# Conditional weight fetches of a mixture-of-experts stage: the next expert is asked for when the current one starts

## The chip, the cores and the metric

The kernel runs on one core of a Trainium2 chip. A time is the device time of one execution in microseconds (us). Before the change three runs gave 460.19, 461.05 and 462.98 us; the median is 461.05.

## The reference, cut to what matters

Three layers follow one another, all in f32: a chunked attention (2 batches, 8 heads, 768 positions, 8 memory keys), a channel mix with three weight matrices, and a mixture of experts whose routing is sticky. The last one is where the change lies:

```python
for b in range(B):
    prev_e = -1
    for s in range(S):
        fresh_e = int(np.argmax(logits[b, s]))
        e = fresh_e if s == 0 or local_gate[b, s] < 0.5 else (prev_e if prev_e >= 0 else fresh_e)
        prev_e = e
        h = np.maximum(x[b, s] @ w1[e], 0.0)          # 512 x 1024
        out[b, s] = softmax(logits[b, s])[e] * (h @ w2[e])   # 1024 x 512
```

So each of 1536 rows passes one of 8 experts, and which one is known only when all logits are there. An expert's two matrices are 2 MB each.

## The kernel before

**Layers.** Attention and channel mix run in four units of 384 rows, on an order that a planner of the program lays out. Each finished row of the channel mix and its expert probability is written to `ys` in DRAM. The expert stage starts while the last unit is routed, at about 255 us.

**Slots.** The rows of an expert are packed into full slots of 128 rows and, for a remainder of at most 64, half slots. `tab_a`, `tab_e`, `tab_b` and `tab_c` (small operations on VectorE and a few on TensorE) work out tables: `ei[0, s]` is the expert of slot `s` (25 entries: 17 full, 8 half), `ei[1, s]` a flag that is 1 where a slot's expert differs from the slot before, `gix` the rows to gather and `six` the rows to store to. With these inputs there are 11 full slots (0 to 10) and 5 half slots. Experts change at slots 4, 8 and 9. Half slots 0 to 4 are taken behind slots 3, 5, 7, 8 and 9 (`HALF_AT`).

**A full slot** (`slot_body`, L1135): the rows come by an indirect DMA of GpSimd's queue into one of three buffers `yg` (`gather`, L855), are transposed on TensorE (`tx`, L866, L871), and go through two matrix products, each as three passes of high and low parts (`s1`, L876; `s2`, L896), with a transpose between (`th`, L889, L893). ScalarE and VectorE split every transposed tile into high and low (`split4`, L862: L863 and L864). `put` (L906) scales the result into `ot[0]`, and `store` (L910) scatters it from GpSimd's queue in the middle of the next slot.

**A half slot** (`half_body`, L1161) does the same for 64 rows without the split, straight from raw weights; all of it, its store, gather and weight fetch included, stands under `tc.If(nh > ...)` (L1183).

**Weights.** Three pairs of raw buffers exist. `raw[0]` holds what the next full slot's expert brings; `raw[1]` and `raw[2]` serve the half slots in turn. `w_fetch(s, k)` (L846) issues matrix `k` of slot `s` from SP's queue with `cond=fv`, the slot's flag: with a flag of 0 the instruction is issued and moves nothing. `w_part(s, part)` (L835) stands under a condition on the same flag; its four `w_piece` calls split a quarter of the raw weights into high (ScalarE, L828) and low (VectorE, L831). In `slot_body(s)` the next slot's first matrix is split between `s2`'s parts (`w_part(s + 1, 0)` and `w_part(s + 1, 1)`), its second in `slot_body(s + 1)` (parts 2 and 3). `h_fetch(h)` (L1067) loads the pair of half slot `h`.

**Order.** From L1051 on the order of each engine's instructions is the program's own (`manual_schedule`). Each queue runs in order: an instruction that waits holds back all behind it. The program's framework places the waits by reads and writes of buffers; a fetch under a condition counts as a write of its buffer. Ahead of the slots SP issues `w_fetch(2, 0)`, `h_fetch(0)` and `h_fetch(1)` (L1130, L1199, L1200). In the slots, SP's order is

```python
w_fetch(s + 1, 1)      # in slot_body(s), behind w_part(s, 3)
w_fetch(s + 2, 0)      # behind w_part(s + 1, 1)
h_fetch(h + 2)         # at the end of half_body(h)
```

Of the kernel before, what the change touches and what calls it, by code (L numbers as in the profile page):

```python
# [9 lines left out]
F32 = mybir.dt.float32  # L10
F32R = mybir.dt.float32r
BF16 = mybir.dt.bfloat16
I32 = mybir.dt.int32
U32 = mybir.dt.uint32
U64 = mybir.dt.uint64
ACTF = mybir.ActivationFunctionType
ALU = mybir.AluOpType
AX = mybir.AxisListType.X
ET = mybir.EngineType

B, H, S, D = 2, 8, 768, 64
CHUNK, LCTX, RCTX, NMEM = 32, 16, 8, 8
DM, DF, NE = 512, 1024, 8
P = 128
# [12 lines left out]
NFULL = 17  # L37
# [3 lines left out]
HALF_AT = (3, 5, 7, 8, 9, 11, 13, 15)  # L41
# [102 lines left out]
def kernel(  # L144
# [15 lines left out]
    nc = tc.nc  # L160
    SCALE = 1.0 / float(D) ** 0.5

    dram = ctx.enter_context(tc.tile_pool(name="dram", bufs=1, space=bass.MemoryType.DRAM))
    cp = ctx.enter_context(tc.tile_pool(name="cp", bufs=1))
    psum = ctx.enter_context(tc.tile_pool(name="psum", bufs=1, space=bass.MemoryType.PSUM))
    ys = dram.tile([B * S + 1, YW], F32, name="ys")


    banks = []
# [50 lines left out]
    stock = {}  # L220
# [21 lines left out]
    ones8 = c_sb[0:NE, 208:336]  # L242
# [444 lines left out]
    for u in range(NU):  # L687
# [4 lines left out]
        if u > 1:  # L692
            for i in range(H // 2):
                att_pair(u * H // 2 + i, T - 19 + 4.0 * i)
            for c in range(NC):
                ev = T - 20 + 2 * (2 * c + 1) + 4.15
# [26 lines left out]

    w1_s, w2_s = wk_s, wv_s
    hbuf, xbuf = wr_s[0:2], wr_s[2:4]
    raw, yg, hv, ot = {}, {}, {}, {}
    tri2 = cp.tile([NE, 16], F32, name="tri2")
    two1 = cp.tile([NE, 1], F32, name="two1")
    gix = cp.tile([P, NSLOT], I32, name="gix")
# [1 line left out]
    sixl = cp.tile([P, 1], I32, name="sixl")  # L731
    ei = cp.tile([1, 2, NSLOT + 3], I32, name="ei")
    fsel = cp.tile([1, 1], I32, name="fsel")

    def open_right():
        att_ctx.close()
        rw = ctx.enter_context(tc.tile_pool(name="rw", bufs=1, side="right"))
        raw[0] = (rw.tile([P, NC, DF], F32, name="raw1_0"), rw.tile([P, NF, DM], F32, name="raw2_0"))
        for k in range(3):
            yg[k] = rw.tile([P, YW], F32, name=f"yg{k}")  # L740
        for k in range(2):
            hv[k] = rw.tile([P, DM], F32, name=f"hv{k}")
# [92 lines left out]
    def w_part(s, part):  # L835
        if s < 2 or s >= NFULL:
            return
        k = (s, body[0] if s > NMIN and body[0] >= NMIN else 0)
        if k not in flag:
            flag[k] = nc.values_load(ei[0:1, 1, s:s + 1], engines=(ET.DVE, ET.Activation),  # L840
                                     min_val=0, max_val=1)
        with tc.If(flag[k]):  # L842
            for c in range(4):
                w_piece(s, part, c, nc.vector)

    def w_fetch(s, k):  # L846

        if s >= NFULL:
            return
        ev = nc.values_load(ei[0:1, 0, s:s + 1], engines=(ET.SP,), min_val=0, max_val=NE - 1)  # L850
        fv = nc.values_load(ei[0:1, 1, s:s + 1], engines=(ET.SP,), min_val=0, max_val=1)
        nc.sync.dma_start(out=raw[0][k], in_=(w1, w2)[k][bass.ds(ev, 1)].rearrange("o (c p) f -> p (o c) f", p=P),
                          cond=fv)

# [19 lines left out]
    def s1(s, g, cs):  # L874
        xh, xl = xbuf[s % 2]
        pb = banks[g]  # L876
        for c in cs:
            wh, wl = w1_s[c][g]
            sl = slice(c * P, (c + 1) * P)
            nc.tensor.matmul(pb, lhsT=xh[:, sl], rhs=wh, start=(c == 0), stop=False)  # L880
            nc.tensor.matmul(pb, lhsT=xh[:, sl], rhs=wl, start=False, stop=False)  # L881
            nc.tensor.matmul(pb, lhsT=xl[:, sl], rhs=wh, start=False, stop=(c == NC - 1))  # L882

    def relu(s, g, on_act):
        if on_act:
            nc.scalar.activation(out=hv[g], in_=banks[g], func=ACTF.Relu)
        else:
            nc.vector.tensor_scalar(out=hv[g], in0=banks[g], scalar1=0.0, scalar2=None, op0=ALU.max)
# [17 lines left out]
    def put(s):  # L906
        nc.scalar.activation(out=ot[0], in_=banks[2 + s % 2], func=ACTF.Copy, scale=yg[s % 3][:, DM:DM + 1])
        nc.vector.tensor_copy(sixl, six[:, s:s + 1])

    def store():  # L910

        nc.gpsimd.indirect_dma_start(out=out, out_offset=bass.IndirectOffsetOnAxis(ap=sixl, axis=0),  # L912
                                     in_=ot[0], in_offset=None, bounds_check=B * S - 1, oob_is_err=False)
# [17 lines left out]
    ef = cp.tile([1, NSLOT + 3], F32, name="ef")  # L931
# [91 lines left out]
    def tab_r():  # L1023
# [4 lines left out]
        nc.vector.tensor_reduce(out=hl[:, NE:], in_=hl[:, 0:NE], op=ALU.max, axis=AX)  # L1028
        nc.vector.tensor_tensor(out=ei[:, 0, NSLOT + 2:], in0=hl[:, NE:], in1=nfull, op=ALU.is_ge)


    u = NU - 1
    T = 20.0 * NU + 0.1
# [8 lines left out]
        (9.0, w_piece, 0, 3, 1, nc.gpsimd), (9.1, w_piece, 0, 3, 2, nc.gpsimd), (9.2, w_piece, 0, 3, 3, nc.gpsimd),  # L1042
        (9.5, tab_a), (10.0, route_c, u), (10.8, th, 0, 1), (11.2, s2, 0, range(0, 4)), (11.3, tab_e), (11.5, tab_b),
        (14.5, s2, 0, range(4, 8)), (15.0, s1, 1, 0, range(0, 4)), (15.1, relu, 1, 0, True), (15.2, tab_c),
        (15.3, gather, 2), (15.4, tab_r),
    ]
    for it in order:
        at(T + it[0], *it[1:])
# [5 lines left out]
    ep = ctx.enter_context(tc.tile_pool(name="ep", bufs=1))  # L1054
    raw[1] = (ep.tile([P, NC, DF], F32, name="raw1_1"), ep.tile([P, NF, DM], F32, name="raw2_1"))
    raw[2] = (ep.tile([P, NC, DF], F32, name="raw1_2"), ep.tile([P, NF, DM], F32, name="raw2_2"))
    for k in range(2):
        ot[k] = ep.tile([P, DM], F32, name=f"ot{k}")
    yh = [ep.tile([P, YW], F32, name=f"yh{k}") for k in range(2)]
    xh4 = [ep.tile([P, 4 * 64], F32, name=f"xh{k}") for k in range(2)]  # L1060
    hh4 = [ep.tile([P, 2 * P], F32, name=f"hh{k}") for k in range(2)]
# [5 lines left out]
    def h_fetch(h):  # L1067
        if h >= NE:
            return
        s = NFULL + h  # L1070
        ev = nc.values_load(ei[0:1, 0, s:s + 1], engines=(ET.SP,), min_val=0, max_val=NE - 1)
        fv = nc.values_load(ei[0:1, 1, s:s + 1], engines=(ET.SP,), min_val=0, max_val=1)
        r1, r2 = raw[1 + h % 2]
        nc.sync.dma_start(out=r1, in_=w1[bass.ds(ev, 1)].rearrange("o (c p) f -> p (o c) f", p=P), cond=fv)
        nc.sync.dma_start(out=r2, in_=w2[bass.ds(ev, 1)].rearrange("o (c p) f -> p (o c) f", p=P), cond=fv)

    def h_gather(h):
        if h < NE:
            nc.gpsimd.indirect_dma_start(out=yh[h % 2], out_offset=None, in_=ys[0:1 + B * S, :],
                                         in_offset=bass.IndirectOffsetOnAxis(ap=gix[:, NFULL + h:NFULL + h + 1], axis=0))  # L1080
# [32 lines left out]
    def h_s2(h, q, ks):  # L1113
        r2 = raw[1 + h % 2][1]
        for k in ks:
            for t in range(2):
                f = 4 * t + 2 * q + k
                for d in range(2):
                    nc.tensor.matmul(banks[2 + h % 2][d * 64:(d + 1) * 64, 0:256],
                                     lhsT=hh4[q][:, k * P + t * 64:k * P + (t + 1) * 64],  # L1120
                                     rhs=r2[:, f, d * 256:(d + 1) * 256], start=(q + k + t == 0), stop=(q + k + t == 3))

    def h_store(h):
        o = ot[1][:, h % 2 * 256:(h % 2 + 1) * 256]
        nc.scalar.activation(out=o, in_=banks[2 + h % 2][:, 0:256], func=ACTF.Copy, scale=yh[h % 2][:, DM:DM + 1])
        s = NFULL + h
        nc.gpsimd.indirect_dma_start(out=outh, out_offset=bass.IndirectOffsetOnAxis(ap=six[:, s:s + 1], axis=0),
                                     in_=o, in_offset=None, bounds_check=2 * B * S - 1, oob_is_err=False)

    w_fetch(2, 0)  # L1130
    put(0)
    nv = nc.values_load(ei[0:1, 0, NSLOT:NSLOT + 1], min_val=0, max_val=NFULL)
    nh = nc.values_load(ei[0:1, 0, NSLOT + 1:NSLOT + 2], min_val=0, max_val=NE)
# [1 line left out]
    def slot_body(s):  # L1135
        body[0] = s
        if s > 1:
            s1(s, 0, range(4))
            w_part(s, 2)
            relu(s, 0, True)  # L1140
        s1(s, 1, range(0, 2))
        th(s, 0)
        s1(s, 1, range(2, 4))
        relu(s, 1, False)
        w_part(s, 3)
        w_fetch(s + 1, 1)
        store()
        gather(s + 2)
        s2(s, range(0, 2))
        if s in HALF_AT:  # L1150
            h_tx(HALF_AT.index(s))
        th(s, 1)
        s2(s, range(2, 4))
        w_part(s + 1, 0)
        tx(s + 1)
        w_part(s + 1, 1)
        w_fetch(s + 2, 0)
        s2(s, range(4, 8))
        put(s)

    def half_body(h):  # L1161
        h_s1(h, 0, range(NC))
        h_relu(0)
        h_s1(h, 1, range(0, 2))
        h_th(h, 0)
        h_s1(h, 1, range(2, NC))
        h_relu(1)
        h_s2(h, 0, range(0, 1))
        h_th(h, 1)
        h_s2(h, 0, range(1, 2))  # L1170
        h_s2(h, 1, range(0, 2))
        h_store(h)
        h_gather(h + 2)
        h_fetch(h + 2)


    def slots(s):
        slot_body(s)
        if s == 1:
            h_gather(0)  # L1180
            h_gather(1)
        if s in HALF_AT:
            with tc.If(nh > HALF_AT.index(s)):  # L1183
                half_body(HALF_AT.index(s))
        if s < NMIN - 1:
            slots(s + 1)
        elif s < NFULL - 1:
            with tc.If(nv > s + 1):
                slots(s + 1)

    def half_rest(h):
        if h < NE:
            with tc.If(nh > h):
                with tc.If(nv < HALF_AT[h] + 1):
                    h_tx(h)
                    half_body(h)
                half_rest(h + 1)

    h_fetch(0)  # L1199
    h_fetch(1)  # L1200
    slots(1)
    nr = nc.values_load(ei[0:1, 0, NSLOT + 2:NSLOT + 3], min_val=0, max_val=1)
# [84 lines left out]
```

## Time and profile before

| What | Value |
|---|---|
| runs | 460.19, 461.05, 462.98 us |
| the profiled execution: own time, span | 459.79 us, 458.0 us |
| TensorE (PE) busy | 414.9 us of the span, 91% |
| VectorE (DVE), ScalarE (ACT), GpSimd (POOL) busy | 251.0, 187.3, 94.2 us |
| mean granted TensorE clock | 0.994 |
| SP's weight loads in the expert stage (`raw`) | 2048 KB each |
| HBM read | 109.40 MB |

The profiled execution's span runs from the first instruction to the last; its own time is 1.8 us longer. A busy PE says that matmuls were in its pipeline, not that it ran at its peak, so what it waited for is read from the lists of waits and from the timeline. SP has no busy time in the table; its instructions are DMA issues, register loads and waits.

### The profile page before, as it was taken

To read this page: it belongs to the slowest core of one execution; us is meant where nothing else is said; L and a number is where in the kernel's file an instruction comes from. 1 tells how busy PE (TensorE), PEld (TensorE's weight loads), DVE (VectorE), ACT (ScalarE), POOL (GpSimd) and SP (SyncE) were. 2 spreads that over 40 slices of the span, in tenths; PEclk is the share of its full clock that TensorE was granted. 3 is DMA by queue.
4 is the path that set the end of the run, shared out by engine and by line. 5 is a ranking of instruction groups with operands and counts; after the bars stand their busy time and mean duration, and the time that the engine had idled before them with its cause. 6 is when DMAs were issued, how large, how long until landed. Compare 5 with 4: busy or idle time off the path is not lost. (4 is left out here: it accounts for less than half of the span.)

```text
span 458.0 us, 10040 instructions
## 1 busy us (share of the span) xinstructions
PE 414.9 (91%) x3827; PEld 351.1 (77%) x3827; DVE 251.0 (55%) x628; ACT 187.3 (41%) x425; POOL 94.2 (21%) x96
## 2 busy tenths in 40 slices
PE   0557999999999999999999899997999999999992
PEld 0436899988999989997999777875786786767672
DVE  4999999835665466646642485225332116474310
ACT  3664995345420553204442231225432126465211
POOL 2312110412300221002320704110130130123030
PEclk9999999999999999999999999999999999999997
DMA  8989860224221020000561026997760897993020
GB/s 277 409 307 333 348 206 1 72 76 134 89 89 36 30 77 2 1 1 24 201 223 37 1 69 216 396 399 299 257 219 10 289 316 253 370 393 124 9 78 24
DMA packets 28096, 76.67 MB, mean 167 GB/s; under 512 B 3819, under 2 KB 3951, under 8 KB 28032
## 3 DMA queue, kind: packets, MB, share of 16 engines
q1 hardware_dynamic: 25216, 67.39, 40.6%
q0 software_dynamic: 2816, 8.47, 5.5%
q8 instruction: 34, 0.56, 0.5%
q14 instruction: 30, 0.25, 0.2%
HBM read 109.40 MB, written 6.69 MB: 254 GB/s over the span
## 5 line engine op out<-in xcount | busy, mean ns | idle before, releaser
L864 DVE TENSOR_TENSOR w<-bank,w 128x512 fp32r<-128x512 f32 x34 | 23.5, 690 | 73.3 <-ACTq L842 57.0
L479 PE MATMUL bank<-xkh,w 128*128 128x384 f32 x128 | 46.9, 366 | 1.2 <-ACT tmp L499 0.9
L211 POOL TENSOR_TENSOR k2l<-tmp,k2h 128x384 fp32r<-128x384 f32 x25 | 27.1, 1085 | 101.0 <-DVE k2h L208 63.8
L480 PE MATMUL bank<-xkl,w 128*128 128x384 f32 x128 | 44.1, 344 | 1.0 <-DVE xkl L211 1.0
L479 PE MATMUL bank<-k2h,w 128*128 128x384 f32 x128 | 44.6, 349 | 0.0
L831 DVE TENSOR_TENSOR w<-raw,w 128x512 fp32r<-128x512 f32 x56 | 35.7, 696 | 15.5 <-ACT w L828 15.2
L481 PE MATMUL bank<-xkh,w 128*128 128x384 f32 x128 | 43.9, 343 | 0.0
L481 PE MATMUL bank<-k2h,w 128*128 128x384 f32 x128 | 43.0, 336 | 0.0
L480 PE MATMUL bank<-k2l,w 128*128 128x384 f32 x128 | 42.9, 335 | 0.0
L863 ACT ACTIVATE w<-bank 128x512 fp32r<-128x512 f32 x34 | 20.3, 597 | 54.3 <-PE bank L893 32.7
L828 ACT ACTIVATE w<-raw 128x512 fp32r<-128x512 f32 x64 | 35.2, 621 | 4.6 <-DMA raw<-in_w_dram 4.3
L880 PE MATMUL bank<-w,w 128*128 128x512 f32 x88 | 36.3, 412 | 0.5 <-issue 0.5
L902 PE MATMUL bank<-w,w 128*128 128x512 f32 x88 | 36.4, 414 | 0.0
L882 PE MATMUL bank<-w,w 128*128 128x512 f32 x88 | 34.6, 394 | 0.0
L881 PE MATMUL bank<-w,w 128*128 128x512 f32 x88 | 34.6, 393 | 0.0
L904 PE MATMUL bank<-w,w 128*128 128x512 f32 x88 | 34.6, 393 | 0.0
L903 PE MATMUL bank<-w,w 128*128 128x512 f32 x88 | 34.4, 390 | 0.0
L381 ACT ACTIVATE Pm<-bank,mx 128x64 f32<-128x64 f32 x96 | 21.3, 322 | 21.8 <-DVE mx L372 21.3
L505 ACT ACTIVATE tmp<-bank 128x384 f32<-128x384 f32 x24 | 11.9, 494 | 41.5 <-PE bank L481 38.8
L479 PEld LDWEIGHTS bank<-xkh,w 128*128 128x128 f32 x128 | 24.8, 194 | 4.4 <-issue 1.9
L480 PEld LDWEIGHTS bank<-xkl,w 128*128 128x128 f32 x128 | 24.8, 194 | 1.4 <-DVE xkl L211 1.4
L481 PEld LDWEIGHTS bank<-xkh,w 128*128 128x128 f32 x128 | 24.7, 193 | 0.0
(214 smaller groups left out, 898.0 us busy)
## 6 DMA issues: line engine op xcount, KB each, us to landing
raw<-in_w_dram SPq DMA_DIRECT2D x36, 2048.0 KB
qk<-in_qkx_dram SPq DMA_DIRECT2D x16, 576.0 KB
vt<-in_vx_dram SPq DMA_DIRECT2D x16, 390.0 KB
w<-in_wk_dram SPq DMA_DIRECT2D x8, 512.0 KB
w<-in_wv_dram SPq DMA_DIRECT2D x8, 512.0 KB
ys<-yr SPq DMA_DIRECT2D x12, 256.0 KB
w<-in_wr_dram SPq DMA_DIRECT2D x4, 512.0 KB
raw<-in_w_dram SPq DMA_DIRECT2D x2, 1024.0 KB
```

The source lines that it names most:

```text
L211: (nc.vector if e == "d" else nc.gpsimd).tensor_tensor(out=o, in0=a, in1=b, op=op)
L479: nc.tensor.matmul(o[:, :UT], lhsT=wh, rhs=xh, start=first, stop=False)
L480: nc.tensor.matmul(o[:, :UT], lhsT=wh, rhs=xl, start=False, stop=False)
L481: nc.tensor.matmul(o[:, :UT], lhsT=wl, rhs=xh, start=False, stop=last)
L828: nc.scalar.activation(out=hi, in_=src, func=ACTF.Copy)
L831: lo_on.tensor_tensor(out=lo, in0=src, in1=hi.bitcast(F32), op=ALU.subtract)
L880: nc.tensor.matmul(pb, lhsT=xh[:, sl], rhs=wh, start=(c == 0), stop=False)
L881: nc.tensor.matmul(pb, lhsT=xh[:, sl], rhs=wl, start=False, stop=False)
L882: nc.tensor.matmul(pb, lhsT=xl[:, sl], rhs=wh, start=False, stop=(c == NC - 1))
L902: nc.tensor.matmul(pb, lhsT=hh[:, sl], rhs=wh, start=(c == 0), stop=False)
L903: nc.tensor.matmul(pb, lhsT=hh[:, sl], rhs=wl, start=False, stop=False)
L904: nc.tensor.matmul(pb, lhsT=hl[:, sl], rhs=wh, start=False, stop=(c == NF - 1))
```

## The change

Five things change.

1. `tab_n`, nine small VectorE operations planned between `gather(2)` and `tab_r`, makes a table `nx`: for a slot whose expert is new, `nx[0, s]` is the next new expert behind it and `nx[1, s]` is 1 if there is one; elsewhere `nx[1, s]` is 0.
2. `w_fetch(s, k)` reads `nx` instead of `ei`, so a fetch "of slot s" loads the expert that follows slot `s`'s, as soon as slot `s`'s own raw weights are split. In `slot_body(s)` the calls are `w_fetch(s, 1)` for `s > 1` and `w_fetch(s + 1, 0)` for `s > 0`.
3. Ahead of the slots SP issues a four-byte DMA from `yg[2]` to a DRAM tile `mark`, which waits for `gather(2)` to land; then `h_fetch(0)`, `w_fetch(0, 0)`, `w_fetch(0, 1)`, `h_fetch(1)`. The early `w_fetch(2, 0)` goes.
4. The half slot's store, gather and fetch leave the condition (`half_end`); its scaling stays in it (`h_put`) and writes one of two tiles `oh`, cleared once by GpSimd.
5. Where a half slot follows a full slot, the full slot's `store()` is issued between the half's arithmetic and `half_end`, and no longer in the next slot.

```diff
     def w_fetch(s, k):
         if s >= NFULL:
             return
-        ev = nc.values_load(ei[0:1, 0, s:s + 1], engines=(ET.SP,), min_val=0, max_val=NE - 1)
-        fv = nc.values_load(ei[0:1, 1, s:s + 1], engines=(ET.SP,), min_val=0, max_val=1)
+        ev = nc.values_load(nx[0:1, 0, s:s + 1], engines=(ET.SP,), min_val=0, max_val=NE - 1)
+        fv = nc.values_load(nx[0:1, 1, s:s + 1], engines=(ET.SP,), min_val=0, max_val=1)
...
+    def tab_n():
+        nm = stock["tmp"][0][0:1, 0:NFULL * NFULL].rearrange("p (a b) -> p a b", b=NFULL)
+        v = stock["tmp"][1][0:1, 0:5 * NFULL].rearrange("p (a b) -> p a b", b=NFULL)
+        rk, fe, fl = v[:, 0:2], v[:, 2:4], v[:, 4]
+        s2d = [1, NFULL, NFULL]
+        nc.vector.tensor_copy(fl, ei[:, 1, 0:NFULL])
+        nc.vector.tensor_tensor_scan(out=rk[:, 0], data0=ones8[0:1, 0:NFULL], data1=fl, initial=0.0, op0=ALU.mult, op1=ALU.add)
+        nc.vector.tensor_scalar(out=rk[:, 1], in0=rk[:, 0], scalar1=1.0, scalar2=None, op0=ALU.add)
+        nc.vector.tensor_tensor(out=fe[:, 0], in0=ef[:, 1:NFULL + 1], in1=fl, op=ALU.mult)
+        nc.vector.tensor_tensor(out=nm, in0=rk[:, 1].unsqueeze(2).to_broadcast(s2d), in1=rk[:, 0].unsqueeze(1).to_broadcast(s2d),
+                                op=ALU.is_equal)
+        nc.vector.tensor_tensor(out=nm, in0=nm, in1=fe[:, 0].unsqueeze(1).to_broadcast(s2d), op=ALU.mult)
+        nc.vector.tensor_reduce(out=fe[:, 1], in_=nm, op=ALU.add, axis=AX)
+        nc.vector.tensor_copy(nx[:, 0], fe[:, 1])
+        nc.vector.scalar_tensor_tensor(out=nx[:, 1], in0=rk[:, 0], scalar=rk[:, 0, NFULL - 1:], in1=fl, op0=ALU.is_lt,
+                                       op1=ALU.mult)
...
-        (15.3, gather, 2), (15.4, tab_r),
+        (15.3, gather, 2), (15.35, tab_n), (15.4, tab_r),
...
+    def h_put(h):
+        nc.scalar.activation(out=oh[h % 2], in_=banks[2 + h % 2][:, 0:256], func=ACTF.Copy,
+                             scale=yh[h % 2][:, DM:DM + 1])
...
-    w_fetch(2, 0)
     put(0)
...
         w_part(s, 3)
-        w_fetch(s + 1, 1)
-        store()
+        if s > 1:
+            w_fetch(s, 1)
+        if s - 1 not in HALF_AT:
+            store()
         gather(s + 2)
...
         w_part(s + 1, 1)
-        w_fetch(s + 2, 0)
+        if s > 0:
+            w_fetch(s + 1, 0)
         s2(s, range(4, 8))
         put(s)
...
         h_s2(h, 1, range(0, 2))
+        h_put(h)
+
+    def half_end(h):
         h_store(h)
         h_gather(h + 2)
         h_fetch(h + 2)
...
             h_gather(1)
+            for k in range(2):
+                nc.gpsimd.memset(oh[k], 0.0)
         if s in HALF_AT:
             with tc.If(nh > HALF_AT.index(s)):
                 half_body(HALF_AT.index(s))
+            store()
+            half_end(HALF_AT.index(s))
...
+    nc.sync.dma_start(out=mark, in_=yg[2][0:1, 0:1])
     h_fetch(0)
+    w_fetch(0, 0)
+    w_fetch(0, 1)
     h_fetch(1)
     slots(1)
```

## Rows read from the trace of the kernel before

**Rows 1.** The page, part 1 and part 2: busy time of PE; DMA share in 40 slices.
```profile
PE 414.9 (91%) x3827; PEld 351.1 (77%) x3827; DVE 251.0 (55%) x628; ACT 187.3 (41%) x425; POOL 94.2 (21%) x96
DMA  8989860224221020000561026997760897993020
```

**Rows 2.** Waits of PE, 215 to 458 us: us in total, times, longest us.
```profile
PE bank L1107 <- ACT hv L1100: 2.8, 1, 2.8
PE bank L893 <- ACT xh L1088: 2.4, 5, 0.5
PE bank L871 <- DMA yg<-ys,gix: 0.5, 1, 0.5
```

**Rows 3.** Timeline of PE, half slot 0: start, us, what, count, idle before and its releaser.
```profile
314.56 2.81 PE L1094 MATMUL bank<-raw,xh 128*64 128x256 f32 x24
320.17 0.44 PE L1107 MATMUL bank<-ident,hv 128*128 128x128 f32 x2 [2.80 <-ACT hv L1100]
```

**Rows 4.** Timeline of PE, half slot 2.
```profile
385.59 2.81 PE L1094 MATMUL bank<-raw,xh 128*64 128x256 f32 x24
388.33 0.44 PE L1107 MATMUL bank<-ident,hv 128*128 128x128 f32 x2
```

**Rows 5.** Timeline of ACT, slots 3, 7 and 9: splits of new weights, and half slot 0.
```profile
310.14 0.60 ACT L863 ACTIVATE w<-bank 128x512 fp32r<-128x512 f32 x1 [0.81 <-PE bank L893]
314.52 2.19 ACT L828 ACTIVATE w<-raw 128x512 fp32r<-128x512 f32 x4 [3.78 <-DMA raw<-in_w_dram]
319.74 0.37 ACT L1100 ACTIVATE hv<-bank 128x256 f32<-128x256 f32 x1
...
381.67 2.20 ACT L828 ACTIVATE w<-raw 128x512 fp32r<-128x512 f32 x4
...
416.26 2.19 ACT L828 ACTIVATE w<-raw 128x512 fp32r<-128x512 f32 x4 [0.25 <-ACT ot L1125]
```

**Rows 6.** Waits of SP's queue, 309 to 316 us.
```profile
SPq L852 <- DMA raw<-in_w_dram: 4.6, 1, 4.6
```

**Rows 7.** Timeline of SP, DMA issues one by one (start us, us).
```profile
277.91 0.40 SPq L1074 DMA_DIRECT2D raw<-in_w_dram  x1
278.61 0.38 SPq L1075 DMA_DIRECT2D raw<-in_w_dram  x1
280.49 5.28 SPq L1074 DMA_DIRECT2D raw<-in_w_dram  x1
...
291.07 0.08 SPq L852 DMA_DIRECT2D raw<-in_w_dram  x1
292.69 0.08 SPq L852 DMA_DIRECT2D raw<-in_w_dram  x1
```

**Rows 8.** The gather's line: issue of `gather(2)` on POOL, and all gathers' landing.
```profile
278.21 0.96 POOL L859 DMA_INDIRECT yg<-ys,gix  x1 [17.45 <-DVE tbs L787]
DMA to landing us min/median/max: 3.4/4.1/7.2
```

**Rows 9.** Stages: us, busy us of PE, PEld, DVE, ACT, POOL, clock, DMA share, GB/s.
```profile
278.00:279.00 1.00, 0.74 (x3) 0.67 (x4) 0.93 (x7) 0.63 (x1) 0.79 (x1) 1.00 0.02 4
280.00:284.00 4.00, 4.00 (x22) 3.34 (x21) 1.38 (x2) 1.01 (x2) 3.09 (x4) 1.00 1.00 366
284.00:290.00 6.00, 5.47 (x27) 4.26 (x26) 1.54 (x3) 1.47 (x3) 0.62 (x2) 1.00 1.02 395
298.00:306.00 8.00, 8.00 (x41) 6.68 (x39) 0.84 (x2) 2.10 (x4) 1.99 (x2) 1.00 1.04 394
```

**Rows 10.** Timeline of DVE where the tables are made.
```profile
273.00 0.16 DVE L1018 TENSOR_TENSOR ei<-ff 1x17 int32<-1x17 f32 x1
273.60 0.20 DVE L1026 SCALAR_TENSOR_TENSOR hl<-c_sb,tot 1x8 f32<-1x8 f32 x1
276.06 0.45 DVE L976 TENSOR_TENSOR Rt<-ohs,c_sb 128x276 bf16<-128x276 f32 x1
```

**Rows 11.** POOL: a store held behind half slot 0's gather.
```profile
333.71 1.45 POOL L912 DMA_INDIRECT out_dram<-ot,sixl  x1 [4.90 <-DMA yh<-ys,gix]
```

More of the change, by code (lines that the diff above doesn't have):

```diff
@@ L166 @@
     ys = dram.tile([B * S + 1, YW], F32, name="ys")
+    mark = dram.tile([1, 1], F32, name="mark")
     banks = []
@@ L725 @@
     hbuf, xbuf = wr_s[0:2], wr_s[2:4]
-    raw, yg, hv, ot = {}, {}, {}, {}
+    raw, yg, hv, ot, oh = {}, {}, {}, {}, {}
     tri2 = cp.tile([NE, 16], F32, name="tri2")
@@ L733 @@
     fsel = cp.tile([1, 1], I32, name="fsel")
+    nx = cp.tile([1, 2, NFULL], I32, name="nx")
     def open_right():
@@ L1057 @@
     for k in range(2):
-        ot[k] = ep.tile([P, DM], F32, name=f"ot{k}")
+        oh[k] = ep.tile([P, 256], F32, name=f"oh{k}")
+    ot[0] = ep.tile([P, DM], F32, name="ot")
     yh = [ep.tile([P, YW], F32, name=f"yh{k}") for k in range(2)]
@@ L1121, in h_s2 @@
                                      rhs=r2[:, f, d * 256:(d + 1) * 256], start=(q + k + t == 0), stop=(q + k + t == 3))
+    def h_put(h):
+        nc.scalar.activation(out=oh[h % 2], in_=banks[2 + h % 2][:, 0:256], func=ACTF.Copy,
+                             scale=yh[h % 2][:, DM:DM + 1])
     def h_store(h):
-        o = ot[1][:, h % 2 * 256:(h % 2 + 1) * 256]
-        nc.scalar.activation(out=o, in_=banks[2 + h % 2][:, 0:256], func=ACTF.Copy, scale=yh[h % 2][:, DM:DM + 1])
         s = NFULL + h
         nc.gpsimd.indirect_dma_start(out=outh, out_offset=bass.IndirectOffsetOnAxis(ap=six[:, s:s + 1], axis=0),
-                                     in_=o, in_offset=None, bounds_check=2 * B * S - 1, oob_is_err=False)
-    w_fetch(2, 0)
+                                     in_=oh[h % 2], in_offset=None, bounds_check=2 * B * S - 1, oob_is_err=False)
     put(0)
@@ L1196, in half_rest @@
                     half_body(h)
+                    half_end(h)
                 half_rest(h + 1)
+    nc.sync.dma_start(out=mark, in_=yg[2][0:1, 0:1])
     h_fetch(0)
+    w_fetch(0, 0)
+    w_fetch(0, 1)
     h_fetch(1)
```

## The prediction

> **What bounds the kernel now.** I read the page first. PE is busy 91% of the span, and in the expert stage the DMA digits stand at 6 to 9 in two stretches, with 0 between them and near the end [rows 1]. So PE sets the pace wherever it is fed, and only its idle time can be won. The list of PE's waits from 215 us on says how much that is: one wait of 2.8 us for a half slot's activation on ACT, one of 0.5 us for gathered rows, and five short ones at every half slot that the change does not touch [rows 2].
>
> The long wait is in half slot 0. From the first matmul (L1094) to the transposes (L1107) it takes 320.17 - 314.56 = 5.61 us, where half slot 2 takes 388.33 - 385.59 = 2.74 us with the same work [rows 3, 4]. That is 2.87 us too long. ACT shows why: it was ready for slot 4's new weights at 310.14 + 0.60 = 310.74, waited 3.78 us for the DMA into `raw`, and began L828 at 314.52; the half slot's activation is queued behind the splits and came at 319.74 [rows 5]. PE goes on 320.17 - 314.52 = 5.65 us after that L828 starts. Without the stall PE would be there at 317.30, so the stall is gone if L828 starts by **311.65**. This one time decides the prediction.
>
> Expert changes at slots 8 and 9 show no DMA in front of L828 [rows 5]: nothing is to be won there.
>
> **The change, part by part.**
>
> *What w_part(4, 0) waits for.* Before, the last write of `raw[0][0]` ahead of the split is `w_fetch(4, 0)`, the transfer itself. After, slot 4's expert is loaded by `w_fetch(0, 0)` and `w_fetch(0, 1)`, but `w_fetch(2, 0)` and `w_fetch(3, 0)` come behind it on the same buffer with a flag of 0. They move nothing, yet they are instructions on SP that wait like writes: the trace has one, `w_fetch(5, 0)`, which stood 4.6 us until the real transfer into its buffer had landed [rows 6]. SP runs in order: `w_fetch(2, 0)` waits for matrix 1 to land, `w_fetch(2, 1)` for matrix 2, and only then comes `w_fetch(3, 0)`, on which the split of slot 4 depends. So ACT is released not by matrix 1 but by **matrix 2 plus one more fetch**. Two such fetches with nothing in the way stand 292.69 - 291.07 = 1.62 us apart [rows 7].
>
> *When the transfers start.* Now SP issues half slot 0's first matrix at 277.91. After, it first waits for `gather(2)`. That was issued at 278.21, under the weights' traffic, and PE had its rows only near 285.4, at the gathers' maximum of 7.2 us; the least any gather took is 3.4 us [rows 8]. With nothing beside it I take 3.4, so 281.6. The four-byte DMA is an issue of 0.1 to 0.4 us (between a skipped and a real one [rows 7]), I take 0.3; a fetch's register loads take what lies between issues at 278.61 and 280.49, 1.9 us [rows 7]. First issue: 283.8. Traffic follows 1.1 us behind an issue (277.91, and almost nothing before 279 [rows 7, 9]): **284.9**, plus d below.
>
> *When matrix 2 lands.* Four transfers of 2.10 MB are 8.39 MB. Indirect DMAs of 128 rows by 2,052 bytes are 0.26 MB each; since the first three of now five early ones have room before 284.9, some 5.5 remain to share the window: 1.45 MB. The full stages run at 366, 395 and 394 GB/s [rows 9]; I take 395, since the 366 has the start in it: 9.84 MB in 24.9 us. The same sum for the present order (five transfers and nine indirect DMAs, 12.85 MB from 279.0) ends at 311.5, and ACT saw the landing at 314.52 [rows 5], so 3.0 us are added for the slowest of the queue's parts and for completion. Matrix 2 lands at 284.9 + 24.9 + 3.0 = 312.8; with 1.6 us for `w_fetch(3, 0)` and 0.1 to wake ACT, L828 starts at **314.5 + d**. Before it was 314.52.
>
> In a sentence by itself: the Trainium skill, "DMA: Bandwidth & Descriptors", Specifications, gives an HBM limit of about 358 GB/s per core, by which the same bytes would take 27.5 us (an estimate) and L828 would start 2.6 us later. The rows at 394 and 395 GB/s contradict that rule, so the sum does not use it.
>
> *What d is.* `tab_n` is nine dependent operations on DVE. The planner places small ones as soon as their inputs are there: `tab_r`, last in program order, ran at 273.60, right behind `ei` at 273.00 and before the operations of `tab_b` that lead to the gather [rows 10]. Six of the nine work on 17 elements and cost about what rows of that size cost, 0.16 to 0.20 us; three work on 289 and are nearest to the 276-element row, 0.45 us [rows 10]. Bounds: 0 if all fall into gaps, 6 x 0.18 + 3 x 0.45 = 2.4 us if all lie on the chain to `gather(2)`. Small ones fit between dependent operations; the three long ones do not quite. I take 0.5 us. So L828 starts at 315.0, **0.5 us later than now**.
>
> *PE's 0.5 us at slot 2.* `gather(2)` without traffic lands some 3.8 us sooner, so this wait goes [rows 2, 8]. But slot 2 lies ahead of the stall, and a stall that ends at a given time swallows it: it counts only if the stall goes too.
>
> *The half slots' transfers outside the condition, and the earlier store.* POOL no longer waits 4.9 us for a half slot's gather before the full slot's store [rows 11]. PE has no wait for a store, and none for a gather but slot 2's [rows 2], so this is worth 0. It would cost only if a gather came after its slot's transposes; gathers are issued over a slot ahead and land in at most 7.2 us [rows 8]. Two memsets on POOL are covered by the same distance.
>
> *The later fetches.* Slot 8's expert will be loaded during slot 4, beside half slot 2's weights, ahead of the slice in which the DMA digits are 0 [rows 1]; its split did not wait even when it was loaded two slots before its use [rows 5]. Slot 9's is asked for at the same places as before. Half slot 1's pair lands some 11 us behind matrix 2 (4.19 MB at 395 GB/s), over a slot before it is used. All worth 0.
>
> *Sum.* 0 (wait at slot 2, swallowed) + 0.5 (stall, d) = +0.5 us on the profiled execution's 459.79, so 460.3. That execution lies 1.26 us under the median of the three runs; on the median it is 461.05 + 0.5, so **461.5**.
>
> **The rivals.**
>
> *A, the stall goes.* Either the skipped fetches do not hold ACT, or the four transfers end 3 us sooner than I think. For it: matrix 1 alone lands some 5 us before matrix 2 (2.10 MB at 395 GB/s), at about 307.5, and that would do; the three terms of the start are small and could each be shorter. Against it: rows 6, and the order on SP. It gives 2.87 + 0.53 - d: at most 3.4 us, 2.9 with d, so 458.2. (That the early fetch is not made at all can be left out: slot 4 would then have no weights.) Chance 16%.
>
> *B, slower.* The same wait, but the block lands later, and every us goes to PE one for one, as soon as L828 starts after 314.52. At the 366 GB/s of the first full stage the bytes take 26.9 us, 2.0 more; d at its upper end is 1.9 more than I took. Either alone gives about 463.5, both 465.4. For it: half slot 0's weights start 6 us later than now, and the sum above has no slack against the present time. Against it: 395 holds over most of the window [rows 9]. Chance 18%. The rule on 358 GB/s has its place here, at 464.2 with d; I give it 1 of these 18, since the rows already exceed it.
>
> *C, the tail or something unseen* (code placed elsewhere, a condition that costs a branch more): 2%.
>
> *The forecast*, L828 within 1.5 us of 315.0 and so 460.0 to 463.0: 64%.
>
> **How the numbers follow.** The time is the forecast's, 461.5. The range reaches down to A near its most (457.8) and up to B with one of its two causes (463.5); beyond are the far parts of B and A, and C, together under 2 in 10. One per cent, 4.6 us, is about what a measurement of this kernel can tell from no change. A at its most gives 3.4 us, so faster by over 1% needs luck in the runs besides: 4%. Slower by over 1% needs both causes of B at once and a little more: 4%. Same: 92%.
>
> **What would show it.** In the changed kernel: traffic starting near 285 instead of 279; `gather(2)` landing in about 3.4 us and PE's L871 without a wait; ACT's L828 of slot 4 at 314 to 316 with an idle of over 3 us in front of it; SP's `w_fetch` waiting for DMAs into `raw` twice for several us before that; and PE still waiting near 320 for the half slot's activation. The forecast is wrong if L828 starts before 312, or if PE's wait at L1107 is gone. It is wrong in kind, not in size, if ACT is released when matrix 1 lands, while matrix 2 is still on its way.

## The result, and the profile after

The changed kernel takes **464.70 us** (median of nine runs, 462.79 to 465.71); beside it the kernel before took 460.97 (nine runs, 459.75 to 462.98). The ratio is 1.0081, with a 95% interval of 1.0059 to 1.0103: slower by 3.7 us, inside the 1% that I had called no change, but above 463.5, the upper end of my range. The profiled execution took 464.70 us (span 462.9), against 459.79 before.

The page after, parts 1 and 2, answers to [rows 1]: PE, the granted clock and the DMA share in 40 slices.

```profile
PE 416.2 (90%) x3827; PEld 351.1 (76%) x3827; DVE 251.8 (54%) x637; ACT 186.8 (40%) x425; POOL 95.2 (21%) x98
...
PE   0557999999999999999999899994999999999992
PEclk9999999999999999999999999998899999999997
DMA  8979950224221120000750015999992850994010
```

As many matmuls as before, but one slice of PE at 4 and two of the clock at 8, all around 320 us. PE's waits, 215 to 463 us (us in total, times, longest), against [rows 2]:

```profile
PE bank L1128 <- ACT hv L1121: 5.9, 1, 5.9
PE bank L895 <- ACT xh L1109: 1.9, 4, 0.5
```

The gather's wait at slot 2 is gone from the list; the wait in half slot 0 has grown from 2.8 to 5.9 us. The timeline of PE there, against [rows 3]:

```profile
313.40 2.81 PE L1115 MATMUL bank<-raw,xh 128*64 128x256 f32 x24
322.13 0.69 PE L1128 MATMUL bank<-ident,hv 128*128 128x128 f32 x2 [5.92 <-ACT hv L1121]
322.75 1.97 PE L1115 MATMUL bank<-raw,xh 128*64 128x256 f32 x8
```

The transposes start 322.13 - 320.17 = 1.96 us later than before. ACT, against [rows 5]:

```profile
308.98 0.60 ACT L865 ACTIVATE w<-bank 128x512 fp32r<-128x512 f32 x1 [0.81 <-PE bank L895]
316.48 2.19 ACT L830 ACTIVATE w<-raw 128x512 fp32r<-128x512 f32 x4 [6.91 <-DMA raw<-in_w_dram]
321.70 0.37 ACT L1121 ACTIVATE hv<-bank 128x256 f32<-128x256 f32 x1
```

L830 (L828 before) waits 6.91 us and starts at 316.48, also 1.96 us later than before: PE inherits it one for one. What released it stands in SP's issues, one by one, against [rows 7]:

```profile
282.16 0.29 SPq L1234 DMA_DIRECT2D mark<-yg  x1
286.10 0.01 SPq L1095 DMA_DIRECT2D raw<-in_w_dram  x1
...
304.37 3.16 SPq L1096 DMA_DIRECT2D raw<-in_w_dram  x1
309.08 0.09 SPq L854 DMA_DIRECT2D raw<-in_w_dram  x1
314.28 0.08 SPq L854 DMA_DIRECT2D raw<-in_w_dram  x1
316.34 0.08 SPq L854 DMA_DIRECT2D raw<-in_w_dram  x1
```

and in SP's waits, 282 to 326 us, against [rows 6]:

```profile
SPq L854 <- DMA raw<-in_w_dram: 3.5, 1, 3.5
```

The trace has matrix 1 landed at 308.89, matrix 2 at 314.13. The last three issues are `w_fetch(2, 0)`, `w_fetch(2, 1)` and `w_fetch(3, 0)`. SP comes to the first only when it is through with the issues of half slot 1's loads, at 307.53, and has made the register loads of the fetch; matrix 1 has just landed by then, and the list has no wait for it. The second waits 3.5 us for matrix 2, and 0.14 us behind the third L830 begins. None of the three moves a byte.

PE then loses a second time. Stages after (us; busy us of PE, PEld, DVE, ACT and POOL with counts; granted clock, DMA share, GB/s):

```profile
314.00:320.00 6.00, 2.21 (x22) 1.17 (x18) 2.85 (x5) 3.52 (x7) 0.00 (x0) 1.00 1.03 399
320.00:322.00 2.00, 0.00 (x0) 0.00 (x0) 2.00 (x5) 2.00 (x5) 0.00 (x0) 0.75 1.05 385
322.00:328.00 6.00, 5.87 (x26) 2.95 (x28) 1.56 (x5) 0.46 (x2) 1.02 (x1) 0.52 0.76 253
328.00:334.00 6.00, 6.00 (x39) 4.32 (x34) 2.50 (x4) 3.15 (x6) 2.13 (x2) 1.00 1.02 421
```

From 322 to 328 us PE is busy at a granted clock of 0.52: nearly all of it on the lower level, 1.2 GHz. Compared matmul by matmul with the trace of before, PE is 0.3 us ahead up to slot 2's transposes, 1.0 to 1.2 ahead behind them (the gather's wait is gone), 1.96 behind at 322.13, and 4.59 behind at 327.9. The last matmul starts 4.25 us later (453.66 against 449.41). In the trace of before the clock never fell there:

```profile
320.00:322.00 2.00, 1.83 (x16) 1.23 (x18) 1.08 (x4) 0.50 (x2) 0.00 (x0) 1.00 0.00 0
322.00:324.00 2.00, 2.00 (x20) 1.09 (x18) 0.52 (x2) 0.00 (x0) 0.00 (x0) 1.00 0.24 33
```

The other rows in turn. The line of the gathers, against [rows 8]:

```profile
DMA to landing us min/median/max: 3.4/3.9/7.4
```

POOL's timeline, `gather(2)` and then the stores at half slot 0, against [rows 8, 11]:

```profile
278.81 0.96 POOL L861 DMA_INDIRECT yg<-ys,gix  x1 [18.28 <-DVE tbs L789]
...
323.52 1.02 POOL L914 DMA_INDIRECT out_dram<-ot,sixl  x1 [20.07 <-ACT hh L1130]
331.56 1.31 POOL L1150 DMA_INDIRECT out_dram<-oh,six  x1 [7.03 <-ACT w L830]
```

`gather(2)` is issued 0.6 us later than before, which is about the cost of `tab_n` (the prediction's d, 0.5; against [rows 10]; 0.7 by itself in e7), and the full slot's store now goes ahead of the half's transfers. The traffic, against [rows 9], runs at 404 GB/s from 298 to 306 us:

```profile
298.00:306.00 8.00, 8.00 (x39) 6.62 (x38) 1.53 (x3) 1.89 (x3) 1.99 (x2) 1.00 1.04 404
```

### The profile page after: what moved, and what is told of

Read it like the earlier page. It is cut to its first block, busy times and chain, and to the rows that moved or that the text cites. A ratio compares the mean times of both kernels' runs of the same rounds, so it can differ in the third digit from the quotient of the medians.

```text
span 462.9 us, 10040 instructions
## 1 busy us (share of the span) xinstructions
PE 416.2 (90%) x3827; PEld 351.1 (76%) x3827; DVE 251.8 (54%) x637; ACT 186.8 (40%) x425; POOL 95.2 (21%) x98
## 5 line engine op out<-in xcount | busy, mean ns | idle before, releaser
L212 POOL TENSOR_TENSOR k2l<-tmp,k2h 128x384 fp32r<-128x384 f32 x25 | 28.4, 1135 | 100.9 <-DVE k2h L209 63.8
L865 ACT ACTIVATE w<-bank 128x512 fp32r<-128x512 f32 x34 | 20.3, 597 | 52.0 <-PE bank L895 27.8
L830 ACT ACTIVATE w<-raw 128x512 fp32r<-128x512 f32 x64 | 35.2, 621 | 8.2 <-DMA raw<-in_w_dram 8.2
L914 POOL DMA_INDIRECT out_dram<-ot,sixl x11 | 11.2, 1018 | 104.5 <-ACTq L844 29.5
L480 PEld LDWEIGHTS bank<-xkh,w 128*128 128x128 f32 x128 | 24.6, 192 | 4.7 <-ACT tmp L500 2.0
```

What stands on the lines that cost most here:

```text
L212: (nc.vector if e == "d" else nc.gpsimd).tensor_tensor(out=o, in0=a, in1=b, op=op)
L480: nc.tensor.matmul(o[:, :UT], lhsT=wh, rhs=xh, start=first, stop=False)
L830: nc.scalar.activation(out=hi, in_=src, func=ACTF.Copy)
```

## The experiments

My theory, **RELEASE**: slot 4's split is freed only by the issue of `w_fetch(3, 0)`. Its rival, **LATE START**: the wait for `gather(2)` ahead of the loads is what makes the split late. And **CLOCK**: the longer stall itself slows what follows it.

**e1: the four-byte DMA taken out**, so that the loads start as before.

```diff
-    nc.sync.dma_start(out=mark, in_=yg[2][0:1, 0:1])
     h_fetch(0)
```

> The changed kernel without the four-byte DMA that waits for gather(2); the order of the fetches stays. First weight issue at about 278 instead of 286, so all four landings come some 6 us earlier (matrix 2 at about 308 instead of 314.1). Theory RELEASE (ACT's split of slot 4 is let go by the flagless w_fetch(3, 0), that is by matrix 2's landing plus 2.3 us): L829 starts at about 310.6, PE's wait at half slot 0 goes (under 0.5 us), the clock stays at 1.00, gather(2) is slow again (about 0.7 us lost at slot 2): about 458. Rival DATA (matrix 1 must land, nothing else matters): matrix 1 at about 302, the stall goes as well, the same 458; this run does not tell the two apart, it tells both from rival OTHER PARTS (the moved stores, the half slots' ends or the new table cost the time), which expects 464 to 465 as before.

458.59 us (11 runs), ratio to the kernel before, here and below, 0.996 (0.994 to 0.9981). SP, PE at slot 2, and ACT:

```profile
278.59 0.40 SPq L1095 DMA_DIRECT2D raw<-in_w_dram  x1
...
286.60 0.66 PE L873 MATMUL bank<-ident,yg 128*128 128x128 f32 x4 [1.94 <-DMA yg<-ys,gix]
...
311.73 2.20 ACT L830 ACTIVATE w<-raw 128x512 fp32r<-128x512 f32 x4
```

With the first load 7.5 us earlier, `w_fetch(3, 0)` is issued at 310.31; L830 begins 4.75 us earlier than in the changed kernel, with no idle time in front of it, and PE's stall is gone. What is paid is the gather, 7.7 us under traffic, and 1.94 us of PE.

**e2: without the idle fetches of slots 2 and 3.** The late start stays; only `w_fetch(2, ...)` and `w_fetch(3, ...)` are left out, which load nothing with these inputs (another routing would need them).

```diff
-        if s >= NFULL:
+        if s >= NFULL or s in (2, 3):
             return
```

> The changed kernel without w_fetch(2, .) and w_fetch(3, .), which move nothing with these inputs; the wait for gather(2), the order and the start of the transfers stay, so matrices 1 and 2 land as in the changed kernel, at about 308.9 and 314.1. Theory RELEASE: ACT's split now waits for matrix 1 alone, which landed before ACT was ready (309.6); the stall and the lower clock go, 464.7 - 3.1 - 2.6 - 2.9 = about 457 (at most 458.5). Rival LATE START (the data come too late because SP waits for gather(2)): L829 still starts at 314 to 316, the time stays within 1 us of 464.7. Rival OTHER PARTS: 464 to 465.

455.99 us (6 runs), ratio 0.9894 (0.9874 to 0.9914). ACT and PE:

```profile
309.61 2.19 ACT L830 ACTIVATE w<-raw 128x512 fp32r<-128x512 f32 x4
...
316.26 0.44 PE L1128 MATMUL bank<-ident,hv 128*128 128x128 f32 x2
```

Matrix 1 lands at 306.83 and matrix 2 when it did (314.15), and still L830 starts 6.87 us earlier, right behind L865 with no wait. So the late start by itself costs nothing, and the release by an idle fetch does. RELEASE is shown; LATE START matters only through it, since either of them taken away (e1, e2) ends the stall.

**e3: PE kept busy in the stall** by 24 matmuls whose result nobody uses.

```diff
         h_s1(h, 1, range(0, 2))
+        if h == 0:
+            for k in range(24):
+                nc.tensor.matmul(banks[7], lhsT=xbuf[1][0][:, 0:P], rhs=w2_s[7][0], start=(k == 0), stop=(k == 23))
         h_th(h, 0)
```

> The changed kernel with 24 extra matmuls of 128x512 (5.4 us at the full clock) on TensorE in half slot 0, between the matmuls of L1115 and the transposes, where PE stood idle for 5.9 us; their result is not used. The wait for ACT stays as it is. Theory CLOCK (the idle time lowered the granted clock to 0.5 from 321.0 to 327.8 and that cost 2.6 us beyond the stall): with PE busy the clock stays at 1.00 and the time FALLS to about 462.0, although work is added. Rival (the 2.6 us come from something else in half slot 0, such as weights that are late or the 64-row matmuls): 464.7 or more.

462.36 us (12 runs), ratio 1.0033 (1.0018 to 1.0048): 2.3 us less than the changed kernel, with work added. PE's timeline:

```profile
316.47 5.78 PE L1192 MATMUL bank<-w,w 128*128 128x512 f32 x24
322.41 0.44 PE L1128 MATMUL bank<-ident,hv 128*128 128x128 f32 x2 [0.16 <-ACT hv L1121]
322.77 1.08 PE L1115 MATMUL bank<-raw,xh 128*64 128x256 f32 x8
```

and the stage from 322 us:

```profile
322.00:328.00 6.00, 5.84 (x47) 3.33 (x46) 1.83 (x5) 0.81 (x4) 1.02 (x1) 1.00 0.70 231
```

The transposes start no earlier (322.41), yet the clock stays at 1.00 and the same eight matmuls take 1.08 us in place of 1.97. That is the clock's part of the loss by itself, and CLOCK is shown.

**e4: slot 4's pair ahead of half slot 0's.**

```diff
-    h_fetch(0)
     w_fetch(0, 0)
     w_fetch(0, 1)
+    h_fetch(0)
     h_fetch(1)
```

> The changed kernel with w_fetch(0, 0) and w_fetch(0, 1) ahead of h_fetch(0) instead of behind it. Matrix 1 and 2 land at about 296.6 and 302.3, half slot 0's pair at about 308.9 and 314.1. Theory RELEASE: w_fetch(3, 0) is issued well before 309, so ACT does not wait; half slot 0's first matrix is needed at about 313.4 and its second at about 317.5, so PE does not wait for them either; no stall, clock 1.00: about 457. Rival HALF LATE (half slot 0's pair is now what comes too late): PE waits 1 to 2 us at L1115 or L1140, 458 to 459.5. Rival OTHER PARTS: 464 to 465.

459.82 us (12 runs), ratio 0.9972 (0.9951 to 0.9994): a miss, near 457 was expected. SP and PE:

```profile
297.31 6.60 SPq L1095 DMA_DIRECT2D raw<-in_w_dram  x1
304.19 3.21 SPq L1096 DMA_DIRECT2D raw<-in_w_dram  x1
308.95 0.09 SPq L854 DMA_DIRECT2D raw<-in_w_dram  x1
310.64 0.08 SPq L854 DMA_DIRECT2D raw<-in_w_dram  x1
312.66 0.08 SPq L854 DMA_DIRECT2D raw<-in_w_dram  x1
...
318.45 0.44 PE L1128 MATMUL bank<-ident,hv 128*128 128x128 f32 x2 [1.98 <-ACT hv L1121]
318.82 1.98 PE L1115 MATMUL bank<-raw,xh 128*64 128x256 f32 x8
```

The pair had landed at 296.25 and 302.00. But SP stood for 6.60 and 3.21 us in the issues of half slot 1's loads, while half slot 0's were still on their way (they landed at 307.72 and 314.53), and came to the idle fetches only at 308.95. PE has no wait for half slot 0's weights, so HALF LATE is not the cause. The split is released by SP reaching `w_fetch(3, 0)`; landing is one of two things that hold SP. The clock adds its part here too: four of the twelve runs have a mean of 0.993 or 0.994 and took 457.71 to 458.64 us, the traced one has 0.990.

**e8: the same with half slot 1's pair moved behind slot 2's work**, which takes the second hold away.

```diff
         slot_body(s)
+        if s == 2:
+            h_fetch(1)
...
-    h_fetch(0)
     w_fetch(0, 0)
     w_fetch(0, 1)
-    h_fetch(1)
+    h_fetch(0)
```

> The changed kernel with slot 4's pair ahead of half slot 0's, and half slot 1's pair issued only behind slot 2's work, so that SP is not held by queued loads when w_fetch(2, 0), w_fetch(2, 1) and w_fetch(3, 0) come. Theory RELEASE WITH ISSUE (slot 4's split waits for the issue of w_fetch(3, 0), which is held by matrix 2's landing and by SP's blocked issues alike): the pair lands at 296 and 302, w_fetch(3, 0) is issued near 304, L830 starts behind L865 near 309.6 without a wait, the clock stays at 1.00, half slot 0's pair lands near 308 and 314 as its first matmuls begin: 456 us, as without the idle fetches. Rival HALF LATE (half slot 0's own weights now end last, and its first matmuls wait 1 to 3 us): 457.5 to 459 us. Rival STILL HELD (something else than landing and issue releases the split): 460 us or more.

**456.21 us** (6 runs), ratio 0.989 (0.9869 to 0.991): it leaves nothing out and beats both kernels. The timelines of SP (`w_fetch(3, 0)`), ACT and PE:

```profile
304.07 0.07 SPq L854 DMA_DIRECT2D raw<-in_w_dram  x1
...
309.89 2.20 ACT L830 ACTIVATE w<-raw 128x512 fp32r<-128x512 f32 x4
...
316.55 0.44 PE L1128 MATMUL bank<-ident,hv 128*128 128x128 f32 x2
```

and the stage:

```profile
314.00:320.00 6.00, 6.00 (x52) 3.52 (x50) 3.32 (x7) 1.99 (x5) 1.02 (x1) 1.00 1.04 399
```

No wait in front of L830, PE busy throughout and the clock at 1.00. Neither rival held.

**e5: the late start alone**, the four-byte DMA put into the kernel before.

```diff
+    mark = dram.tile([1, 1], F32, name="mark")
...
+    nc.sync.dma_start(out=mark, in_=yg[2][0:1, 0:1])
     h_fetch(0)
```

> The kernel before, with the four-byte DMA on gather(2) ahead of h_fetch(0) and nothing else. Theory LATE START (the wait for gather(2) moves every load of SP's queue back by about 7 us, and costs whatever the release of slot 4's split costs): the first weight is issued near 284.8 in place of 277.9, matrix 1 of slot 4 (the fifth transfer in this order) lands near 319.4, L828 starts near 319.5 in place of 314.5, PE's wait in half slot 0 grows by 5 us and the clock falls behind it, as it did in the changed kernel after a gap of 6.3 us (2.6 us): 468 to 469 us against 461. Rival NEUTRAL (the DMA costs only what gather(2)'s 0.5 us gives back): 461 us, and L828 at 314 to 315.

466.97 us (6 runs), ratio 1.0123 (1.0102 to 1.0144). ACT and PE:

```profile
318.30 2.19 ACT L829 ACTIVATE w<-raw 128x512 fp32r<-128x512 f32 x4 [8.40 <-DMA raw<-in_w_dram]
...
323.95 0.69 PE L1108 MATMUL bank<-ident,hv 128*128 128x128 f32 x2 [7.44 <-ACT hv L1101]
```

A start 6.7 us later makes the split 3.8 us later, 1.2 less than expected, and the time is 1 us under the expected 468. Where the split needs the fifth of the queued transfers, the late start is dear; in e2, where nothing holds the split, it is free.

**e6: parts 4 and 5 of the change undone.**

```diff
-        if s - 1 not in HALF_AT:
-            store()
+        store()
...
                 half_body(HALF_AT.index(s))
-            store()
-            half_end(HALF_AT.index(s))
+                half_end(HALF_AT.index(s))
```

> The changed kernel, with the half slot's store, gather and fetch put back under its condition, and the full slot's store back in the next slot's middle (parts 4 and 5 of the change undone, but for the scaling's own tile). Theory RELEASE (all of the 3.7 us lost comes from slot 4's split, the clock behind it and the tail): 464.7 us, within 0.7, with L830 at 316.5 and the clock at 0.5 behind the gap as before. Rival OTHER PARTS (the transfers outside the condition or the order of the stores carry part of the loss, the 0.7 us of the tail at least, or bring a gain that the loss hides): it differs from 464.7 by more than 1 us, and the last matmul or the tail behind it says where.

464.01 us (6 runs), ratio 1.0063 (1.0042 to 1.0085), which overlaps the changed kernel's. In the traces the two run together to 322.13 (PE at 322.04 here), and differ by 1.0 us behind it as the lower clock ended at 325.67 here and at 327.81 there. The parts are worth nothing that these runs can tell.

**e7: `tab_n` alone**, in the kernel before, its table unused (the function and its tile `nx` are added as in the change; the planner's line is shown).

```diff
-        (15.3, gather, 2), (15.4, tab_r),
+        (15.3, gather, 2), (15.35, tab_n), (15.4, tab_r),
```

> The kernel before, with the nine operations of tab_n planned where the changed kernel has them, their table unused. The prediction's term d was 0.5 us (0 to 2.4). Theory SMALL d: gather(2) is issued about 0.6 us later and what PE loses ahead of slot 2 is swallowed by the stall at half slot 0, since the weights start as before: 460.8 to 461.4 us. Rival DEAR TABLE (the operations delay the last unit's work or the gathers by their full 2.4 us): 462 to 463.5 us.

460.20 us (12 runs), ratio 0.998 (0.996 to 1.0): no slower, and a little under the 460.8 to 461.4 that I expected. PE at slot 2 and at half slot 0:

```profile
286.83 0.66 PE L872 MATMUL bank<-ident,yg 128*128 128x128 f32 x4 [2.15 <-DMA yg<-ys,gix]
...
320.76 0.44 PE L1127 MATMUL bank<-ident,hv 128*128 128x128 f32 x2 [2.13 <-ACT hv L1120]
```

PE waits 1.62 us more for the gather than in the trace of before, is 1.3 us late ahead of the stall and only 0.59 behind it: the stall swallows what lies ahead. The 0.59 comes from the loads, which do not start as before: the first is issued at 278.60 and not at 277.91, slot 4's first matrix lands at 315.03 and not at 314.44, and ACT's split follows it. So d, some 0.7 us here, moves the loads too.

**e9, e10, e11: the kernel before, three more times.** A puzzle was left: in e4 a wait of 1.98 us was followed by the lower clock, in the trace of before one of 2.80 was not. And before's runs form two groups by mean clock: of 28, 13 had 0.993 to 0.996 and took 459.27 to 460.79 us, 11 had 0.989 to 0.991 and took 460.87 to 462.70 (four more had a lower one). A mean does not say where the clock was low: e1, whose trace has no stall at half slot 0, has two runs of 11 at 0.989, and e7's runs do not sort this way (459.31 us with 0.989, 461.29 with 0.996, the traced one). Three more traces look.

> The kernel before, unchanged, profiled once more. Its runs so far lie in two groups, near 459.3 to 460.9 us with a mean granted clock of 0.993 to 0.996, and near 461.2 to 462.9 us with 0.989 to 0.991; the one traced so far is of the first. Theory CLOCK IN SOME RUNS (the stall of 2.8 us at half slot 0 lowers the clock in some executions and not in others): an execution with a mean near 0.990 shows a clock of 0.5 for 3 to 4 us behind the stall at 320 us and its last matmul some 1.7 us later than 449.4. Rival ELSEWHERE: the clock stays at 1.00 there, and what is longer lies in another stage.

> The same kernel a second time, since one execution may fall in either group. Theory CLOCK IN SOME RUNS: with a mean near 0.990 a clock of 0.5 for 3 to 4 us behind the stall at 320 us and 461 to 463 us; with 0.993 or more none, and 459 to 461 us. Rival ELSEWHERE: the clock at half slot 0 is the same in both groups.

> The same kernel a third time. Theory CLOCK IN SOME RUNS: with a mean near 0.990 a clock of 0.5 for 3 to 4 us behind the stall at 320 us and 461 to 463 us; with 0.993 or more none, and 459 to 461 us. Rival ELSEWHERE: the clock at half slot 0 is the same in both groups.

All three have the mean clock of the second group: 462.19, 463.30 and 461.31 us with 0.989, 0.989 and 0.990. In e9, PE's timeline:

```profile
320.33 0.60 PE L1107 MATMUL bank<-ident,hv 128*128 128x128 f32 x2 [2.55 <-ACT hv L1100]
320.86 1.98 PE L1094 MATMUL bank<-raw,xh 128*64 128x256 f32 x8
```

and a stage of it:

```profile
322.00:324.00 2.00, 2.00 (x12) 0.96 (x10) 0.42 (x1) 0.00 (x0) 0.00 (x0) 0.53 0.08 12
```

The lower clock is there in the very kernel from which I forecast, behind a wait that is even shorter (2.55 us), and from the transposes until the clock is back PE falls back 1.63 us against the first trace (e10 and e11: 1.58). Another 0.8 us of e10 lie elsewhere, around a second wait for ACT at 412 us. CLOCK IN SOME RUNS holds.

## Why the prediction was wrong

**Right: the wait that decides, and what releases it.** `gather(2)` at the shortest landing and PE without a wait for it, an idle fetch waiting for matrix 2, L830 released by `w_fetch(3, 0)` and not at matrix 1's landing, PE's wait near 320 still there: these came as written. Behind it stands a rule of the Trainium skill, "DMA: Bandwidth & Descriptors", Anatomy of one DMA: a wait in front of a DMA is taken by the engine that issues it, not by the DMA engines. The trace agrees: SP stood 3.5 us in front of a fetch that moves nothing. The parts taken at zero were zero as far as e6 can tell, and what PE gains or loses ahead of a stall is swallowed by it (a lead of 1.2 us in the changed kernel, the lag in e7).

**Wrong in size: "L828 starts at 315.0, 0.5 us later than now".** It was 316.48, 1.96 later. Of the 1.48 us between, 0.83 lie before matrix 2 (landed at 314.13, forecast 313.3) and 0.65 behind it: I took 1.6 + 0.1 us from landing to ACT; it was 0.15 for `w_fetch(2, 1)` to go, 2.06 to the next fetch and 0.14 to wake ACT. The start's own terms were less exact than their sum: from the `mark` issue to the first weight it took 3.94 us, not 2.2 (2.28 in e3 and e6), and the weights' first bytes moved at about 287, 1.6 us behind the forecast's 285.4; but the traffic ran at 404 GB/s for a stretch, not 395. 316.48 lies just inside the 1.5 us that I had allowed, but outside the 314 to 316 that I had named as a sign.

**Missed, without effect on the time: what holds SP.** I had SP wait twice for DMAs into `raw`, first for matrix 1. It waited once. Up to 307.53 it stood in the issues of half slot 1's loads, 6.65 and 3.16 us long, and it came to `w_fetch(2, 0)` just behind matrix 1's landing. My account had no term for an issue that blocks, though [rows 7] has one of 5.28 us. Here matrix 2 landed later still, so the hold cost nothing, which was luck: in e4 it decides.

**The step that failed: the path behind the stall, which had no term for the clock.** I priced a later L828 one for one and put all that follows it at nothing; no case of mine held a lower clock, and it is the larger part. In the profiled pair PE lost 1.96 us at the stall and 2.63 behind it, drifted back 0.34, and the tail (from the last matmul's start to the end) was 0.72 longer: 4.97 in all, as the executions differ by 4.91. The tail is scatter: it is 8.55 us in the first trace, and the kernel before itself has 8.52 in e11 and 9.77 in e10.

A rule bears on the missing step: "TensorE: Matmul & The Clock Gate" of the Trainium skill, Part 1, says that a PE that has gone idle drops to half its clock and gets it back only by work. The changed kernel's 0.52 and e3's 1.00 agree. Not every wait is followed by it (the list at the end). I had read the page of before, whose PEclk never fell behind its own stall of 2.8 us, and concluded nothing from it; e9 to e11 show that this trace was of the luckier group.

**Missing with it: the base.** I put +0.5 on the median as if only the stall could move. But the kernel before pays about 1.6 us of clock in some of its runs (e9 to e11; 11 of those 28, if their mean tells), the changed kernel 2.6 in the one traced. The changed kernel's mean clock was 0.986 or 0.987 in eight of nine runs, as low as in that trace. By the traces 1.96 + 2.63 - 0.34 is 4.25; less about 0.4 x 1.6 = 0.6 that the median of before already holds, some 3.6, an estimate, against 3.7 measured. The same base is part of why e2 and e8 gain 4.8 and 5.3 us and not only the 3.4 of rival A: their last matmuls start 4.28 and 4.00 us before that of the first trace, and without the stall the median's 0.6 us of clock are not lost either. What is left in e8, 0.7 us, is open.

Rival B had the direction and, by another cause, nearly the time, which was luck: matrix 2 landed 0.8 us late and not 2, and d was some 0.6. Its price "one for one" was right at the stall and stopped there.

## What to carry to other kernels

A fetch under a false condition moves nothing, but it waits in its queue and counts as the last write of its buffer: put it behind what the consumer needs next, or leave the queue free to reach it. When a change lengthens an idle stretch of PE, price the matmuls behind it at half clock too; and take more than one trace of the kernel before as the base, above all where its runs' times and mean clocks fall into groups. What wins is the order: the pair whose consumer stalls goes first, and nothing large is queued ahead of the instruction that releases it (e8).

## What the hardware showed

- **The clock behind a short idle is not decided by its length alone.** Waits of 1.98, 2.18, 2.55 and 2.60 us (e4, e11, e9, e10) were followed by 0.5; 2.80 (the first trace) and 2.13 (e7) were not. All of 5.8 us and more were (the changed kernel, e5, e6). What decides among the short ones stays open.
- **Issuing a large load can hold the queue's engine for long**: 6.60 us for one issue in e4; the same load, asked for in e8 when only half slot 0's pair was on its way, took 0.39.
- **`gather(2)` takes 3.4 us ahead of the weights' traffic (the changed kernel) and 7.7 beside it** (e1), and waiting for it costs the kernel nothing where no release hangs on the loads' end (e2).
